# The last 64 rows of the projections' low weights, multiplied for two tiles at once on halves of the array

## The chip, the cores and the metric

The kernel runs on one core of one Trainium2 chip. Its engines work side by side, each through its own queue in order: PE (TensorE, the matrix array, with its weight loads listed apart as PEld), ACT (ScalarE), DVE (VectorE), POOL (GpSimd) and SP (SyncE, which here only issues DMAs). The metric is the device time of one execution in microseconds (us); lower is better. Before the change it is 1898.07 us, the median of three runs (1897.98 to 1898.41).

## The reference

Four blocks over x of 2048 tokens by 448 features, each added to x: attention with 16 heads of 28 features, a gated feed-forward block with 1792 hidden features, and both once more with the same weights.

```python
x = x + attention(layernorm(x), wqkv, wo)
x = x + (sigmoid(g) * u) @ w_down        # g, u = layernorm(x) @ w_gate, w_up
x = x + attention(layernorm(x), wqkv, wo)
x = x + (sigmoid(g) * u) @ w_down
```

The change lies in the first step of attention, `qkv = layernorm(x) @ wqkv`, a product over 448 features that gives 448 columns each for queries, keys and values. It runs twice, once in each layer.

## The kernel before

**Split numbers.** The products run in 16-bit floats, with each operand cut into a high and a low part: hi(w)·hi(x) + hi(w)·lo(x) + lo(w)·hi(x). The 448 features are three blocks of 128 rows and a tail of 64. For the tail one operand holds two things: `tail` has hi(x) in rows 0 to 63 and lo(x) in rows 64 to 127, and the tail's weights stand twice, in rows 0 to 63 and again in rows 64 to 127. One matmul with the high weights gives hi·hi + hi·lo, a second one with the low weights gives lo·hi (and lo·lo). So an output tile takes 3 × 3 + 2 = 11 matmuls.

**Blocks and tiles.** The tokens are cut into four blocks (b = 0 to 3) of 512. For each block `qk(b, ...)` makes seven output tiles of 128 features by 512 tokens: queries and keys, 896 rows in all. Tile i goes into a PSUM bank, one of four in turn. What follows a tile is written out in this order: ACT copies it as 16-bit `hl` (L756), DVE computes the rest (L757), ACT squares it (L759), DVE takes the larger of the two halves' squares (L761), SP stores `hl` to DRAM (L764), and then the tile's entry of the list `fill` is called. That entry is work for later blocks: statistics (`norm`), scaling and transposing (`squares`), storing and reading back (`store`, `gather`), cutting into high and low (`ready`, which is `part` for two row blocks each: L218 and L223 on ACT, L219 and L224 on DVE). Layer 0 has `add` there too, sums of squares of other weights (L957). All of it goes into the same in-order queues of ACT, DVE, POOL and SP.

**The norm products.** Each tile's squares go through a small matmul into a bank of query norms (L735) or key norms (L738). They wait in the queue `late`: from tile 3 on one is taken per tile, and `finish()` (called `fin`) takes those left, three of them, and has DVE reduce the two banks to `peaks` (L774). PE meets `fin` at a place fixed in its program: for layer 0 after the third tile of values of block 1, after the second tile of queries and keys of block 3 (for block 2, through `before`), and after the first tile of values of block 2 (for block 3); for layer 1 after the second tile of values of block 0, and then as in layer 0 (block 1 after its second tile of values).

**Values.** `vals(b, ...)` makes four tiles of 128 tokens by 448 features for a block, 11 matmuls each (L586 to L591), which ACT copies (L792). Block 0's and block 1's come right after their queries and keys; blocks 2 and 3 have theirs after block 3's queries and keys. The third tile of block 3 goes to bank 0 in layer 0 and bank 7 in layer 1, and DVE copies it (L794). Behind it start the scores of attention (L1202), which write groups of three banks each, in a fresh set of banks laid over the same memory.

In layer 0 block 0 is special: its matmuls are interleaved with the making of the weights (`along`), and blocks 0 and 1 are turned on PE (`turned_high`, `turned_low`) instead of through DRAM.

Of the kernel before, what the change touches and what calls it, by code (L numbers as in the profile page):

```python
# [25 lines left out]
NT = S // P  # L26
NB = 4
TB = NT // NB
W = TB * P
# [11 lines left out]
PS = 2.0 ** -13  # L41
# [77 lines left out]
def interleaved_layers(ctx: ExitStack, tc: tile.TileContext, x_in, wqkv, wo, w_gate, w_up,  # L119
                       w_down, out):  # L120
    nc = tc.nc
# [6 lines left out]
    big = Slots(spool, "s", N_SLOTS)  # L128
# [22 lines left out]
    def bank(i, name):  # L151
        return psum(f"bank{i}", name, [P, 512])


    x = cpool.tile([P, NT, D], F32, name="x")
# [62 lines left out]
        nc.scalar.copy(hi, raw)  # L218
        nc.vector.tensor_tensor(lo, raw, hi, op=ALU.subtract)  # L219

    def split_tail(tail, raw):

        nc.scalar.copy(tail[0:64], raw[0:64])  # L223
# [39 lines left out]
    class Block:  # L263
# [97 lines left out]
        def part(self, kt):  # L361

            raw = self.raw[:, kt, :].rearrange("p (i t c) -> p t i c", i=4, t=TB)
            order = "p (t i c) -> p t i c"
            if kt < 3:
                hi = self.hi[:, kt, :].rearrange(order, t=TB, i=4)
                lo = self.lo[:, kt, :].rearrange(order, t=TB, i=4)
                split(hi, lo, raw)
            else:
                split_tail(self.tail.rearrange(order, t=TB, i=4), raw)  # L370
                big.put(self.raw)

        def steps(self):
# [149 lines left out]
        def turned_high(self, kts=range(4), engine=None):  # L523
            for kt in kts:
                if kt not in self.pt:
                    continue
                to, pt = ((self.hi[:, kt, :], self.pt[kt]) if kt < 3 else
                          (self.tail[0:64], self.pt[kt][0:64]))
                if engine is nc.vector:
                    nc.vector.tensor_copy(to, pt)  # L530
                else:
                    nc.scalar.copy(to, pt)

        def turned_low(self, kts=range(4)):
            for kt in kts:
# [13 lines left out]
            else:  # L549
                big.put(self.all)  # L550

    def by_features(pm, blk, wh, wl, first_tile=None):

        order = [(wh, blk.hi), (wh, blk.lo), (wl, blk.hi)]
        terms = [(w(kt), x[:, kt, :]) for kt in range(3) for w, x in order]
        tails = [(w(3), blk.tail) for w in (wh, wl)]
        if first_tile == 0:
            terms = terms[0::3] + terms[1:5:3] + terms[2::3] + terms[7:8] + tails
        elif first_tile == 1:
            terms = terms[0::3] + terms[1::3] + tails[0:1] + terms[2::3] + tails[1:2]  # L560
        else:
            terms += tails
        for i, (w, x) in enumerate(terms):
            nc.tensor.matmul(pm, w, x, start=(i == 0), stop=(i == len(terms) - 1))  # L564

    def of_halves(pm, w, blk, k, first):

# [14 lines left out]
    def by_tokens(pm, hi, lo, tail, w, kts=range(4)):  # L582

        for kt in kts:
            if kt == 3:
                nc.tensor.matmul(pm, tail, w[:, 0, 3, :], start=False, stop=False)  # L586
                nc.tensor.matmul(pm, tail, w[:, 1, 3, :], start=False, stop=True)  # L587
                continue
            nc.tensor.matmul(pm, hi(kt), w[:, 0, kt, :], start=(kt == 0), stop=False)  # L589
            nc.tensor.matmul(pm, hi(kt), w[:, 1, kt, :], start=False, stop=False)  # L590
            nc.tensor.matmul(pm, lo(kt), w[:, 0, kt, :], start=False, stop=False)  # L591
# [120 lines left out]
    def project(layer, wq, begun):  # L712


        values = [big.get("val", [P, TB, H, VC]) for _ in range(NB)]
# [4 lines left out]
                nc.gpsimd.memset(v[:, :, :, DH:DH + 1], 1.0)  # L720

        peaks = cpool.tile([H, 2, NB], F32, name=f"peaks{layer}", tag="peaks", bufs=2)
        evac = [0]

        def qk(b, blk, fill, before):
            pn = [bank(4 + 2 * (b % 2), "qnorm"), bank(5 + 2 * (b % 2), "knorm")]
            late = deque()

            def rows_of_heads(i):

                return ind[:, i:i + P // H, :].rearrange("p a h -> p (a h)")

            def norm_products(i, sq):
                if i <= 3:
                    nc.tensor.matmul(pn[0][:, 0:W // 2], rows_of_heads(i), sq[:, 0:W // 2],  # L735
                                     start=(i == 0), stop=(i == 3))
                if i >= 3:
                    nc.tensor.matmul(pn[1][:, 0:W // 2], rows_of_heads(1 + i), sq[:, 0:W // 2],  # L738
                                     start=(i == 3), stop=(i == 6))
                qrt.put(sq)  # L740

            for i in range(7):
                pm = bank(evac[0] % 4, "qkp")
                evac[0] += 1
                c = slice(i * P, (i + 1) * P)
                by_features(pm, blk, lambda kt: wq.qk[0][:, kt, c],
                            lambda kt: wq.qk[1][:, kt, c], i if layer == 0 and b == 0 else None)
                if layer == 0 and b == 0:
                    along[i]()
                if i == 1 and before:  # L750
                    before()
                if len(late) == 3:
                    late.popleft()()
                hl = qrt.get("qkhl", [P, 2, W], F16)
                sq = qrt.get("sq", [P, W], BF16)
                nc.scalar.activation(hl[:, 0, :], pm, AF.Copy, scale=PS)  # L756
                nc.vector.scalar_tensor_tensor(hl[:, 1, :], pm, PS, hl[:, 0, :], op0=ALU.mult,  # L757
                                               op1=ALU.subtract)
                nc.scalar.activation(sq, hl[:, 0, :], AF.Square)  # L759

                nc.vector.tensor_tensor(sq[:, 0:W // 2], sq[:, 0:W // 2], sq[:, W // 2:W],  # L761
                                        op=ALU.max)
                n = slice(b * W, (b + 1) * W)
                nc.sync.dma_start(qk_scr[c, :, n], hl)  # L764
                qrt.put(hl)
                late.append(lambda i=i, sq=sq: norm_products(i, sq))
                if i < len(fill) and fill[i]:
                    fill[i]()

            def finish():  # L770
                while late:
                    late.popleft()()
                for i in range(2):
                    nc.vector.tensor_reduce(peaks[:, i, b:b + 1], pn[i][0:H, 0:W // 2], axis=AX.X,  # L774
                                            op=ALU.max)
            return finish

        def values_product(pv, blk, j, kts=range(4)):
            t = slice(j * P, (j + 1) * P)
            by_tokens(pv[:, 0:D], lambda kt: blk.hi[:, kt, t], lambda kt: blk.lo[:, kt, t],  # L780
                      blk.tail[:, t], wq.v, kts)

        def vals(b, blk, after, tiles=range(TB), at=None, begun=None):
            for j in tiles:
                pv = begun or bank(evac[0] % 4 if at is None else at, "vp")
                evac[0] += 1
                values_product(pv, blk, j, range(2, 4) if begun else range(4))
                if j in after:
                    after[j]()
                v, pv = values[b][:, j, :, 0:DH], pv[:, 0:D].rearrange("p (h d) -> p h d", d=DH)  # L790
                if at is None:
                    nc.scalar.activation(v, pv, AF.Copy, scale=PS)  # L792
                else:
                    nc.vector.tensor_scalar(v, pv, PS, None, op0=ALU.mult)  # L794
            if tiles[-1] == TB - 1:
                blk.drop()

        def tile0():
            wq.low_cols(0, P, D)
            wq.measure(1)  # L800
            ones_of_values()
# [10 lines left out]
        def nothing():  # L812
# [989 lines left out]
    wq = WeightsQKV()  # L1802
    wq.tiles()
    first = Block(0)
    begun = [first]
# [41 lines left out]
    for layer in range(LAYERS):  # L1847
        values, heads, last_values = project(layer, wq, begun)
        gate = WeightsGated()
        outs = attend(layer, values, heads, last_values, gate, wq.keep)  # L1850
        mlp_first = out_project(outs, gate)
        wq = WeightsQKV()
# [5 lines left out]
        begun = gated(layer, mlp_first, gate, before_next)  # L1858
# [28 lines left out]
```

## Time and profile before

| | us |
|---|---|
| median of three runs | 1898.07 |
| the profiled execution | 1896.41 |
| its span, first to last instruction | 1894.6 |
| PE busy | 1888.2 (100%) |
| DVE busy | 1431.0 (76%) |
| ACT busy | 1383.4 (73%) |
| POOL busy | 231.5 (12%) |
| layer 0, first query/key matmul to first score | 12.43 to 118.35 |
| layer 1, the same | 954.15 to 1056.30 |

A row of the timeline gives the start, the time taken, the engine and source line, the output and input, and how many instructions are merged in the row; square brackets hold the idle time just before and what ended it. Matmuls overlap, so the pitch from one start to the next is what a matmul costs PE, not the time taken that its row shows. A row of the stretches gives, for a piece of the span, its length and each engine's busy time and number of instructions, then the granted PE clock and the load of the DMA engines.

### The profile page before, as it was taken

What the parts mean: (1) busy time and instruction counts of PE and PEld (TensorE: products, weight loads), DVE (VectorE), ACT (ScalarE), POOL (GpSimd) and SP (SyncE); (2) the same over time, 40 slices, a digit from 0 to 9 for tenths busy, and PEclk for the clock granted to TensorE, in tenths of its full rate; (3) what the DMA queues carried; (4) which work ended last, traced back from release to release, by engine and by line L of the source; (5) the groups of instructions that cost most, each with busy time, mean ns of one, the idle gap of its engine ahead of it and who ended that gap; (6) DMA issues with size and microseconds to landing.
All of it is one profiled execution on the core that took longest, in us unless ns stands there. A gap on an engine that the chain in (4) does not pass through costs nothing. (4 is left out here: it accounts for less than half of the span.)

```text
span 1894.6 us, 56258 instructions
## 1 busy us (share of the span) xinstructions
PE 1888.2 (100%) x24254; PEld 1334.2 (70%) x24254; DVE 1431.0 (76%) x2835; ACT 1383.4 (73%) x1772; POOL 231.5 (12%) x453
## 2 busy tenths in 40 slices
PE   9999999999999999999999999999999999999999
PEld 4455555556566799999954566766556677999998
DVE  7758989898976688787563487787778676887664
ACT  5569999999993566555345799999999745665541
POOL 3023112222101111111100000000000020121110
PEclk9999999999999999999999999999999999999999
DMA  7676444344323566646734321122121135666553
GB/s 250 194 212 164 130 137 130 108 118 130 102 81 116 191 205 236 230 182 237 251 97 132 90 52 47 32 52 52 30 49 53 61 127 169 218 253 223 209 208 142
DMA packets 109570, 269.81 MB, mean 142 GB/s; under 512 B 12926, under 2 KB 66526, under 8 KB 109184
## 3 DMA queue, kind: packets, MB, share of 16 engines
q0 software_dynamic: 31776, 158.51, 23.5%
q1 hardware_dynamic: 77200, 107.38, 20.2%
q8 instruction: 192, 3.15, 0.7%
q14 instruction: 66, 0.54, 0.1%
q10 hardware_dynamic: 336, 0.23, 0.0%
HBM read 207.88 MB, written 50.85 MB: 137 GB/s over the span
## 5 line engine op out<-in xcount | busy, mean ns | idle before, releaser
L1217 ACT ACTIVATE prob_s<-sc 128x1536 f32<-128x1536 f32 (+1 forms) x657 | 887.8, 1483 | 6.7 <-PE sc L1202 5.9
L1253 PE MATMUL acc<-prob_s,val_s 128*32 128x256 f32 (+3 forms) x7700 | 571.7, 383 | 0.0
L1202 PE MATMUL sc<-qp_s 114*32 114x512 f16 x7868 | 554.9, 379 | 0.0
L579 PEld LDWEIGHTS <-gu_s 128*128 128x128 f16 x4368 | 426.8, 98 | 46.9
L1202 PEld LDWEIGHTS <-qp_s 114*32 114x32 f16 x8192 | 277.3, 95 | 199.0 <-issue 82.7
L1253 PEld LDWEIGHTS acc<-prob_s,val_s 128*32 128x32 f32 x7700 | 276.7, 110 | 139.2 <-issue 12.4
L579 PE MATMUL chain<-xwide_s,gu_s 128*128 128x256 f16 x2016 | 247.5, 273 | 0.0
L1533 PE MATMUL dnp<-dn_s,hparts_s 128*128 128x224 f16 x2016 | 225.2, 259 | 0.0
L1533 PEld LDWEIGHTS <-hparts_s 128*128 128x128 f16 x2016 | 194.0, 98 | 4.4
L1233 DVE SCALAR_TENSOR_TENSOR power_q<-power_q,expo_q 128x512 f32<-128x512 f32 x243 | 168.2, 692 | 8.3
L1606 ACT COPY one_q<-chain 128x256 f32<-128x256 f32 x224 | 82.4, 371 | 121.1 <-PE chain L579 120.4
L1622 DVE TENSOR_TENSOR one_q<-side,one_q 128x512 f32<-128x512 f32 x112 | 72.2, 687 | 103.3 <-PE side L579 100.7
L579 PE MATMUL side<-xshort_s,gu_s 128*128 128x256 f16 x1120 | 140.6, 273 | 0.0
L564 PE MATMUL qkp<-xhl_s,wqk_s 128*128 128x512 f16 x616 | 137.9, 379 | 0.7 <-ACT wqk_s L231 0.2
L564 PEld LDWEIGHTS <-wqk_s 128*128 128x128 f16 x616 | 60.1, 98 | 70.4 <-ACT wqk_s L231 1.1
L1418 POOL DMA_DIRECT2D gu_s<-gu_parts x104 | 56.0, 538 | 431.9 <-PE side L579 418.1
L1282 DVE STREAM_TRANSPOSE oturned_q<-acc 128x512 f32<-128x512 f32 x32 | 22.9, 716 | 97.0 <-PE acc L1253 96.9
L1253 PE MATMUL acc<-power_q,val_s 128*32 128x256 f32 (+3 forms) x300 | 94.2, 396 | 0.0
L579 PE MATMUL side<-xwide_s,gu_s 128*128 128x256 f16 x672 | 91.7, 273 | 0.0
L1486 ACT CAST hparts_s<-hsums_q 128x256 f16<-128x256 f32 (+1 forms) x136 | 65.0, 494 | 30.1 <-DVE hsums_q L1498 20.4
L756 ACT ACTIVATE qkhl_q<-qkp 128x512 f16<-128x512 f32 x56 | 33.2, 593 | 73.2 <-PE qkp L564 69.6
L1633 ACT ACTIVATE one_q<-one_q 128x512 f32<-128x512 f32 x56 | 35.2, 629 | 63.9 <-DVE one_q L1622 63.9
(218 smaller groups left out, 2333.2 us busy)
## 6 DMA issues: line engine op xcount, KB each, us to landing
gu_s<-gu_parts POOLq DMA_DIRECT2D x104, 800.0 KB, 6.0
dn_s<-dn_parts POOLq DMA_DIRECT2D x42, 784.0 KB, 7.6
qp_s<-qk_scr SPq DMA_DIRECT2D x96, 224.0 KB
qk_scr<-qkhl_q SPq DMA_DIRECT2D x56, 256.0 KB
gu_parts<-pack_s POOLq DMA_DIRECT2D x14, 800.0 KB, 3.8
xt_scr<-xs_s SPq DMA_DIRECT2D x48, 224.0 KB
xraw_s<-xt_scr SPq DMA_DIRECT2D x12, 768.0 KB
qp_s<-qk_scr SPq DMA_DIRECT2D x64, 112.0 KB
```

The lines of the kernel that those rows point to most:

```text
L564: nc.tensor.matmul(pm, w, x, start=(i == 0), stop=(i == len(terms) - 1))
L579: nc.tensor.matmul(pm, a, x, start=(first and i == 0), stop=(i == len(terms) - 1), skip_group_check=True)
L1202: nc.tensor.matmul(ps[32 * j:32 * j + 32, :], hd.k[:, keys], hd.q[:, qb * W:(qb + 1) * W], start=True, stop=True, tile_position=(0, 32 * j))
L1217: nc.scalar.activation(prob[:, 0:n, :], ps[:, 0:n, :], AF.Exp, scale=exp_scale)
L1233: nc.vector.scalar_tensor_tensor(p, p, c[k], y, op0=ALU.add, op1=ALU.mult)
L1253: nc.tensor.matmul(acc[qb * VC:(qb + 1) * VC, s], v[:, kc % TB, h, :], probs[c * NB + qb][:, s], start=(kc == 0 and a == 0), stop=(kc == N ...
L1418: queue.dma_start(self.gu[-1][m], gu_parts[p, m])
L1486: nc.scalar.copy(to[:, :, 0], a)
L1533: nc.tensor.matmul(pm, a[:, x, t], w[:, p, y], start=(begin and n == 0 and (j == 0 or alone)), stop=(n == 2), skip_group_check=True)
L1606: nc.scalar.copy(to, pm)
L1622: nc.vector.tensor_tensor(one[m], side[m], one[m], op=ALU.add)
L1633: nc.scalar.activation(out, v, AF.Sigmoid, scale=gate_scale)
```

## The change

The second tail matmul, with the low weights, needs only hi(x), that is 64 rows. It is now made with 64 rows: for even tiles with rows 0 to 63 (`tail`), for odd tiles with rows 64 to 127, for which a copy of the tail's hi(x) is put into rows 64 to 127 of a new operand `upper`. `on_halves` issues these matmuls for a group of four tiles, even and odd in turn. For that, the first four tiles of queries and keys of a block first get 10 matmuls each, one tile after the other; then come the four half matmuls; then the four tiles' copies with what belongs to them, and only then tiles 4 to 6, with 11 matmuls as before. The same holds for the four tiles of values of a block. Left as they were: queries, keys and values of block 0 in layer 0, and values of block 3.

Four tiles are now open at once, so six banks go round (0 to 3, 6, 7; block 0 of layer 0 keeps four), and both norms of a block share one bank (4 or 5). `late` gives one norm product per tile from tile 4 on, so that four are left for `fin`. The third values tile of block 3 goes to bank 0 in both layers.

```diff
-    def split_tail(tail, raw):
+    def split_tail(tail, upper, raw):
         nc.scalar.copy(tail[0:64], raw[0:64])
+        nc.scalar.copy(upper[64:128], raw[0:64])
         nc.vector.tensor_tensor(tail[64:128], raw[0:64], tail[0:64], op=ALU.subtract)
...
-            self.all = big.get("xhl", [P, 7, W], F16)
+            self.all = big.get("xhl", [P, 8, W], F16)
+            self.upper = self.all[:, 7, :]
...
+                if kt == 3 and self.b > 0:
+                    nc.scalar.copy(self.upper[64:128], pt[0:64])
...
+    def on_halves(outs, high, low):
+        for i, pm in enumerate(outs):
+            r = slice(64 * (i % 2), 64 * (i % 2) + 64)
+            nc.tensor.matmul(pm, *(v[r] for v in (high(i), low(i))), start=False, stop=True)
...
-            terms += tails
+            terms += tails if ends else tails[:1]
...
-        evac = [0]
+        order = deque([0, 1, 2, 3] if layer == 0 else [0, 1, 2, 3, 6, 7])
+        def next_bank(name):
+            order.rotate(-1)
+            return bank(order[-1], name)
+        def alone(b):
+            return layer == 0 and b == 0
...
-            pn = [bank(4 + 2 * (b % 2), "qnorm"), bank(5 + 2 * (b % 2), "knorm")]
+            if layer == 0 and b == 1:
+                order.extend([6, 7])
+            both = bank(4 + b % 2, "norms")
+            pn = [both[:, 0:W // 2], both[:, W // 2:W]]
...
+            def copies(i, pm):
...
                 if i < len(fill) and fill[i]:
                     fill[i]()
+            group = []
+            for i in range(7):
+                pm = next_bank("qkp")
+                c = columns(i)
+                single = alone(b) or i > 3
+                by_features(pm, blk, lambda kt: wq.qk[0][:, kt, c],
+                            lambda kt: wq.qk[1][:, kt, c], i if alone(b) else None, single)
+                if alone(b):
+                    along[i]()
+                if i == 1 and before:
+                    before()
+                if len(late) >= 3:
+                    late.popleft()()
+                if single:
+                    copies(i, pm)
+                    continue
+                group.append(pm)
+                if i == 3:
+                    on_halves(group, lambda i: wq.qk[1][:, 3, columns(i)],
+                              lambda i: blk.upper if i % 2 else blk.tail)
+                    for j, pm in enumerate(group):
+                        copies(j, pm)
...
+            grouped = not alone(b) and b < NB - 1
             for j in tiles:
+                pvs[j] = begun or (next_bank("vp") if at is None else bank(at, "vp"))
+                values_product(pvs[j], blk, j, range(2, 4) if begun else range(4), not grouped)
                 if j in after:
                     after[j]()
+                if not grouped:
+                    copy_values(b, j, pvs[j], at)
+            if grouped:
+                on_halves([pvs[j][:, 0:D] for j in tiles],
+                          lambda j: (blk.upper if j % 2 else blk.tail)[:, j * P:(j + 1) * P],
+                          lambda j: wq.v[:, 1, 3, :])
+                for j in tiles:
+                    copy_values(b, j, pvs[j], at)
...
-        vals(3, blks[3], {}, [2], 0 if layer == 0 else 7)
+        vals(3, blks[3], {}, [2], 0)
```

The inner part of `copies` is the code of L754 to L768, unmoved, the call of `fill[i]` at its end included.

More of the change, by code (lines that the diff above doesn't have):

```diff
@@ L369, in part @@
             else:
-                split_tail(self.tail.rearrange(order, t=TB, i=4), raw)
+                split_tail(self.tail.rearrange(order, t=TB, i=4),
+                           self.upper.rearrange(order, t=TB, i=4), raw)
                 big.put(self.raw)
@@ L561, in by_features @@
         else:
[L562 removed]
+            terms += tails if ends else tails[:1]
         for i, (w, x) in enumerate(terms):
[L564 removed]
+            nc.tensor.matmul(pm, w, x, start=(i == 0), stop=(ends and i == len(terms) - 1))
     def of_halves(pm, w, blk, k, first):
@@ L580, in of_halves, with by_tokens @@
                              stop=(i == len(terms) - 1), skip_group_check=True)
-    def by_tokens(pm, hi, lo, tail, w, kts=range(4)):
+    def by_tokens(pm, hi, lo, tail, w, kts=range(4), ends=True):
         for kt in kts:
@@ L734, in norm_products, with columns @@
                 if i <= 3:
-                    nc.tensor.matmul(pn[0][:, 0:W // 2], rows_of_heads(i), sq[:, 0:W // 2],
-                                     start=(i == 0), stop=(i == 3))
+                    nc.tensor.matmul(pn[0], rows_of_heads(i), sq[:, 0:W // 2],
+                                     start=(i == 0), stop=(i == 3), skip_group_check=True)
                 if i >= 3:
-                    nc.tensor.matmul(pn[1][:, 0:W // 2], rows_of_heads(1 + i), sq[:, 0:W // 2],
-                                     start=(i == 3), stop=(i == 6))
+                    nc.tensor.matmul(pn[1], rows_of_heads(1 + i), sq[:, 0:W // 2],
+                                     start=False, stop=(i == 6), skip_group_check=True)
                 qrt.put(sq)
[L742 to L753, printed above, removed]
+            def columns(i):
+                return slice(i * P, (i + 1) * P)
+            def copies(i, pm):
+                c = columns(i)
                 hl = qrt.get("qkhl", [P, 2, W], F16)
```

26 lines of the change are left out of this document (14 added, 12 removed).

## Prediction

> **What bounds the kernel.** The page comes first: whose time is the span?
>
> ```profile
> PE 1888.2 (100%) x24254; PEld 1334.2 (70%) x24254; DVE 1431.0 (76%) x2835; ACT 1383.4 (73%) x1772; POOL 231.5 (12%) x453
> ```
>
> PE is never free, so a matmul less is time less, and a wait on PE is time more. But 76% for DVE is a mean over the span, so I read next the stretches that the change touches: here the queries and keys of layer 0's block 3, and the whole of layer 1's block 0.
>
> ```profile
> 84.85:105.21 20.36, 20.07 (x102) 9.70 (x100) 19.16 (x41) 11.05 (x20) 0.00 (x0) 1.00 0.37 124
> 954.15:980.29 26.14, 25.97 (x131) 12.63 (x129) 19.64 (x45) 12.28 (x21) 2.43 (x4) 1.00 0.30 89
> ```
>
> The numbers behind the length are PE, PEld, DVE, ACT, POOL. DVE is busy for 19.16 of 20.36 us in the one and 19.64 of 26.14 in the other: in places DVE is a second bound. Third, the timeline of PE at the places where `fin` stands:
>
> ```profile
> 90.27 0.27 PE L738 MATMUL knorm<-sq_q,ind 128*128 128x256 bf16 x1 [0.29 <-DVE sq_q L761]
> ...
> 104.88 0.49 PE L738 MATMUL knorm<-sq_q,ind 128*128 128x256 bf16 x3
> ...
> 975.47 0.38 PE L738 MATMUL knorm<-sq_q,ind 128*128 128x256 bf16 x2
> 976.03 0.27 PE L738 MATMUL knorm<-sq_q,ind 128*128 128x256 bf16 x1 [0.17 <-DVE sq_q L761]
> ```
>
> In two of them PE waits already, 0.29 and 0.17 us, for the last square's maximum on DVE. DVE is just in time there, and the change starts DVE's chain later.
>
> **What it saves on PE.** Pitches first.
>
> ```profile
> 954.15 9.66 PE L564 MATMUL qkp<-xhl_s,wqk_s 128*128 128x512 f16 x44
> ```
> ```profile
> 1058.47 0.35 PE L590 MATMUL vp<-wv_s,xhl_s 128*128 128x448 f16 x1
> 1058.66 0.35 PE L591 MATMUL vp<-wv_s,xhl_s 128*128 128x448 f16 x1
> 1058.95 0.83 PE L1202 MATMUL sc<-qp_s 114*32 114x512 f16 x12
> 1059.71 0.36 PE L589 MATMUL vp<-wv_s,xhl_s 128*128 128x448 f16 x1
> ```
>
> 44 matmuls in 9.66 us, of which the last one's tail is about 0.16, are 0.216 each; a values matmul is 0.19 (1058.66 less 1058.47). The last three rows also show the array changing shape: scores use it in strips of 32 columns. Going in, the first score starts at 1058.95, 0.10 later than the pitch from 1058.66 would have it; coming back, three rounds at 0.216 after 1058.95 end at 1059.60, and the next full matmul starts at 1059.71: 0.11. The twelve scores go in rounds of four side by side.
>
> No row shows halves of rows. A pair of half matmuls costs between one matmul (0.216: side by side) and two (0.432: one after the other). I take the lower end, since four column strips, the nearest row, run side by side. By the Trainium skill ("TensorE: Matmul & The Clock Gate", Part 3, Packing small matmuls) tiles on different rows overlap with about 4 ns between starts; the pair would be 0.22, and the sum as it stands. Changing the shape costs between 0 and the 0.21 above; I take 0.21 per group, since it is a change of shape as those are.
>
> A group of queries and keys turns four matmuls into two pairs: 2 × 0.216 less 0.21 is 0.22 us; there are seven groups (three in layer 0, four in layer 1): 1.6. A group of values: 2 × 0.19 less 0.21 is 0.17; five groups (blocks 1, 2 and then 0, 1, 2): 0.85. Together 2.4 us, 0.13%: that is the whole gain. With free changes of shape it would be 4.9.
>
> **What it moves.** Tile 0 to 3's copies, and the four `fill` entries between them, now wait for the group's end instead of their own tile's. ACT's and DVE's queues are in order, so everything behind moves too. ACT's pitches:
>
> ```profile
> 956.72 0.60 ACT L756 ACTIVATE qkhl_q<-qkp 128x512 f16<-128x512 f32 x1 [28.84 <-PE qkp L564]
> ...
> 988.24 1.14 ACT L218 CAST xhl_s<-xraw_s 128x512 f16<-128x512 f32 x2 [1.74 <-DMA xraw_s<-xt_scr]
> 989.28 0.59 ACT L756 ACTIVATE qkhl_q<-qkp 128x512 f16<-128x512 f32 x1
> 989.90 0.63 ACT L759 ACTIVATE sq_q<-qkhl_q 128x512 bf16<-128x512 f16 x1
> 990.44 0.60 ACT L218 CAST xhl_s<-xraw_s 128x512 f16<-128x512 f32 x1
> 990.95 0.61 ACT L223 CAST xhl_s<-xraw_s 64x512 f16<-64x512 f32 x1
> 991.47 0.58 ACT L756 ACTIVATE qkhl_q<-qkp 128x512 f16<-128x512 f32 x1
> ```
>
> A tile's copy and square are 1.15; two L218 1.04; an L218 and the tail's L223 1.03, to which `upper` adds a copy like L223, 0.51, seven in all, on an ACT that is busy for half of these stretches. A tile's copy begins 0.41 after its last matmul starts (956.72 less 954.15 less ten pitches).
>
> **Layer 1, block 0: the largest term.**
>
> ```profile
> 964.71 0.69 DVE L757 SCALAR_TENSOR_TENSOR qkhl_q<-qkp,qkhl_q 128x512 f16<-128x512 f32 x1
> ...
> 975.13 0.65 DVE L757 SCALAR_TENSOR_TENSOR qkhl_q<-qkp,qkhl_q 128x512 f16<-128x512 f32 x1
> 975.70 0.27 DVE L761 TENSOR_TENSOR sq_q<-sq_q 128x256 bf16<-128x256 bf16 x1
> ```
>
> DVE's work on tile 3 starts at 964.71; behind it stand `b2.norm`, tile 4, two `squares`, tile 5, two `squares`, tile 6, and the last maximum ends at 975.97: 11.3 us with hardly a gap, and after the change the same instructions in the same order. Now when does it start? The group's 40 matmuls end at 954.15 + 8.64; with the change of shape the first half matmul starts at 962.89, tile 0's copy at 963.30. ACT then does tiles 0 and 1 (2.30), two L218 (1.04), tile 2 (1.15), L218, L223 and `upper` (1.54), tile 3's copy (0.60): DVE can start tile 3 at 969.95, 5.2 us later than before. Its chain ends at 981.2. PE asks for it after 962.89 + 0.43 + 0.11, tiles 4 to 6 with a norm product each (3 × 2.48) and two values tiles of ten matmuls (3.8): at 974.7. PE waits 6.5 us, in two gaps (tile 5's norm product comes between). Against the old time the norm product is 5.2 us late; behind it two values tiles took 4.2 us and now take 4.4 (20 matmuls, two pairs, two changes of shape). **Block 0 ends 5.4 us later.**
>
> **The rest of layer 1.** Blocks 1 to 3 have no DVE work between tiles 3 and 6, so ACT sets the pace: tile 6's maximum comes about 0.3 us before PE asks in blocks 1 and 3, and 2 us before in block 2. No wait: −0.4, −0.2, −0.4. Block 2's rows come back from DRAM 5.2 us later, as all before them; the row of 988.24 becomes 993.5, and ACT needs them at 997.1 (two tiles after the group). Then the bank of the third values tile:
>
> ```profile
> 1056.30 0.40 PE L1202 MATMUL sc<-qp_s 114*32 114x512 f16 x4
> ```
> ```profile
> 1056.40 0.62 DVE L794 TENSOR_SCALAR val_s<-vp 128x448 f32<-128x448 f32 x1 [6.18 <-PE vp L587]
> ```
>
> With bank 7 the first score starts while DVE still copies. If the scores' first group lies over bank 0, as its place as the first allocated says, it starts after 1057.02: +0.75 (bounds: 0 and 0.75). Layer 1: 5.4 − 1.0 + 0.75 = **+5.15**.
>
> **Layer 0.** The same with DVE's rows here:
>
> ```profile
> 50.02 0.68 DVE L757 SCALAR_TENSOR_TENSOR qkhl_q<-qkp,qkhl_q 128x512 f16<-128x512 f32 x1
> ...
> 62.63 1.29 DVE L219 TENSOR_TENSOR xhl_s<-xraw_s,xhl_s 128x512 f16<-128x512 f32 x2 [0.57 <-ACT xhl_s L218]
> 63.84 0.69 DVE L757 SCALAR_TENSOR_TENSOR qkhl_q<-qkp,qkhl_q 128x512 f16<-128x512 f32 x1
> ...
> 84.13 2.08 DVE L957 CUSTOM_DVE_ANT_0 junk_s<-raw_s,sums 128x1792 bf16<-128x1792 f32 x1
> ...
> 89.33 0.69 DVE L757 SCALAR_TENSOR_TENSOR qkhl_q<-qkp,qkhl_q 128x512 f16<-128x512 f32 x1
> ...
> 96.79 1.13 DVE L957 CUSTOM_DVE_ANT_0 junk_s<-raw_s,sums 128x896 bf16<-128x896 f32 x1
> ```
> ```profile
> 65.27 0.49 PE L738 MATMUL knorm<-sq_q,ind 128*128 128x256 bf16 x3
> ```
>
> Block 1 (from 41.86): tile 1's DVE work moves from 50.02 to 52.8 (group end 50.6, copy 51.0, one tile 1.15, copy 0.6); of these 2.75 us the 0.57 of waiting before 62.63 and a little more are taken up, tile 6's goes from 63.84 to 65.94, its norm product to 66.9, where PE stood at 65.27 before. With the fourth values tile and its pairs (2.5) the block ends at 69.5 instead of 67.7: **+1.8**.
>
> Block 2: its group ends at 78.2. ACT's row (tiles 0, 1, two L218, tile 2, L218, L223, `upper`, tiles 3, 4) brings tile 4's DVE work to 86.4 and the first `add` from 84.13 to 87.2, 3.07 later. From there it is DVE's old row (two `add` and a tile, 5.2 us, to 89.33), so the last norm product goes from 90.27 to 93.3. PE asks at 90.7, so it waits 2.6. Cumulative **+3.07**.
>
> Block 3: PE leaves `fin` at 93.45; two tiles (4.3) and a change of shape later the group's pairs start at 97.9, tile 0's DVE work at 98.9. Behind it in DVE's queue: tiles 0 to 6 at 0.8 (5.20 less two `add` of 2.2), and three `add` of 2.2, 1.3 and (128 columns more) 1.4: the last maximum at 109.4. PE asks at 107.6, waits 1.8, leaves at 109.55; before, the three products of 104.88 ended their pitches at 105.2. Cumulative **+4.35**; the rest (three values tiles, the start of attention) is as long as before, 6.3 us.
>
> **Free things.** The shared norm bank: PE writes both norms before DVE reads either. Banks: in each place the bank that PE takes next was read by DVE over 1 us before. SP's stores of `hl` come in bunches; the gathers behind them are covered as above, in layer 0's block 2 with 0.7 us to spare.
>
> **Sum.** 4.35 + 5.15 = +9.5 us. The profiled execution had 1896.41 (span 1894.6 and 1.8 around it), 1.66 below the median; added to the median: **1907.6**. What a measurement of this kernel tells from no change is about 0.2%, 3.8 us.
>
> **Rivals.**
> *Not slower (0.07).* DVE has over 6 us to spare in layer 1's block 0 (19.64 of 26.14); if its queue were not held up, PE would ask and find. Then only the 2.4 us gain and the bank's 0.75 stay: 1896.4. It decides at the last maximum of that block: it must end by 974.7, not 981.2. Against it: the spare time lies ahead of the group's end, where DVE has nothing to do.
> *The pairs run one after the other (0.12).* Then 0.43 more in seven groups and 0.38 in five, 4.9: 1912.5. The strips of the scores speak against it.
> *The clock falls in the waits (0.12).*
>
> ```profile
> 1.25 4.88 PE L261 MATMUL still<-still_q 128*128 128x512 f16 x11 [1.25 <-DVE warm L179]
> ```
>
> The first eleven matmuls of the kernel took 4.88 us, where eleven take 2.54 at the pitch above: a PE that comes from rest loses 2.3 us. If the gaps of about 3 us in layer 1's block 0 (and one of 2.6 in layer 0) do this, it is 2.3 to 4.6 more: 1910 to 1912. The Trainium skill ("TensorE: Matmul & The Clock Gate", Part 1) has the clock halved after an idle window of about 3.4 us; by it the gaps, each just about that long and cut by norm products, would mostly escape.
> *Some waits are shorter than worked out (0.09)*: half of them leaves +3 to 4, about 1902.
>
> **How the numbers follow.** The forecast has 0.60: 1907.6, its own range 1904.5 to 1910 (0.75 for the bank, 2 for waits worked out to some tenths each). The range goes from 1903.0 to 1912.8, up to the serial pairs. Slower by over 0.2% (above 1901.9): 0.60 + 0.12 + 0.12 + most of 0.09, and some of the first rival's cases, 0.89; same 0.08; faster, which needs free changes of shape and no wait at all (1893.9), 0.03.
>
> **What the changed profile would show.** In the list of waits, PE for DVE's squares (L761) with 12 to 14 us in all instead of 0.5, the longest gaps of about 3 us in layer 1's block 0. DVE's busy time as before, idle for some 9 us in each block's group. Half matmuls in pairs within 0.22 us, 0.1 us free on either side. The first score of layer 0 some 4.4 us later, that of layer 1 9.5. Wrong would be: norm products without waits, or waits on a DMA or a bank that I called free.

## The result and the profile after

The changed kernel takes 1910.57 us, the median of 6 executions (1908.95 to 1914.19); the kernel before took 1897.82 beside it (1897.32 to 1898.41, 6 executions). The ratio is 1.0068, with a 95% interval of 1.0057 to 1.0078: 12.75 us slower. The forecast was 1907.6, with a range of 1903.0 to 1912.8. The profiled execution has 1911.11 us and a span of 1909.3, 14.7 more than the one of before.

The engines' line of the page, after:

```profile
PE 1889.6 (99%) x24254; PEld 1326.4 (69%) x24254; DVE 1432.0 (75%) x2835; ACT 1382.5 (72%) x1779; POOL 231.4 (12%) x453
```

The work is as before, within 1.5 us on every engine (PE's weight loads, listed apart, take 7.8 us less), and the instructions are as many, but for the seven copies to `upper` on ACT. So nearly all of the 14.7 us is time in which PE stands still; what it does more slowly hides in its busy time, which should have fallen. In the list of PE's waits after, two entries stand out (in all, times, longest):

```profile
PE norms L763 <- DVE sq_q L779: 11.7, 7, 3.4
PE sc L1254 <- DMA qp_s<-qk_scr: 1.3, 1, 1.3
```

The first was 0.5 us before the change, the second was not there. A third entry, PE's wait for the turning of the first tokens (`turn`) at the kernel's start, has 1.0 us instead of 0.2; it lies between 0.2 and 2.0 us in the twelve traces and is 1.6 us in experiment 7, which is the kernel before with `fin` moved, so it is no part of the change. Where do the seven waits of the first entry stand? The timeline of PE, the norm products that waited and the rows behind two of them:

```profile
65.33 0.27 PE L763 MATMUL norms<-sq_q,ind 128*128 128x256 bf16 x1 [0.20 <-DVE sq_q L779]
67.33 0.27 PE L763 MATMUL norms<-sq_q,ind 128*128 128x256 bf16 x1 [1.74 <-DVE sq_q L779]
67.44 0.35 PE L603 MATMUL vp<-wv_s,xhl_s 128*128 128x448 f16 x1
67.63 0.54 PE L604 MATMUL vp<-wv_s,xhl_s 128*128 128x448 f16 x1
...
71.08 0.55 PE L562 MATMUL vp<-wv_s,xhl_s 64*128 64x448 f16 x4
...
95.78 0.27 PE L763 MATMUL norms<-sq_q,ind 128*128 128x256 bf16 x1 [2.56 <-DVE sq_q L779]
...
111.21 0.27 PE L763 MATMUL norms<-sq_q,ind 128*128 128x256 bf16 x1 [0.53 <-DVE sq_q L779]
112.01 0.27 PE L763 MATMUL norms<-sq_q,ind 128*128 128x256 bf16 x1 [0.53 <-DVE sq_q L779]
...
984.75 0.27 PE L763 MATMUL norms<-sq_q,ind 128*128 128x256 bf16 x1 [3.44 <-DVE sq_q L779]
987.70 0.37 PE L763 MATMUL norms<-sq_q,ind 128*128 128x256 bf16 x1 [2.68 <-DVE sq_q L779]
987.87 0.58 PE L603 MATMUL vp<-wv_s,xhl_s 128*128 128x448 f16 x1
988.24 0.58 PE L604 MATMUL vp<-wv_s,xhl_s 128*128 128x448 f16 x1
...
992.70 0.35 PE L603 MATMUL vp<-wv_s,xhl_s 128*128 128x448 f16 x1
992.89 0.35 PE L604 MATMUL vp<-wv_s,xhl_s 128*128 128x448 f16 x1
```

They are the `fin` of blocks 1, 2 and 3 of layer 0 and of block 0 of layer 1, the places that the prediction named. But read on behind the waits: from 987.87 the values matmuls follow each other at 0.373 us instead of 0.19, for thirteen of them, until 992.70. The same from 67.63 to 71.08. In the stretches (length, then PE, PEld, DVE, ACT, POOL, then the granted clock, the third number from the end):

```profile
66.00:72.00 6.00, 4.67 (x17) 1.67 (x17) 3.31 (x7) 1.14 (x3) 0.00 (x0) 0.72 0.77 196
88.30:112.12 23.82, 20.20 (x102) 9.39 (x100) 20.60 (x44) 12.26 (x22) 0.00 (x0) 1.00 0.30 100
960.27:994.61 34.34, 28.22 (x132) 12.54 (x130) 22.18 (x50) 10.80 (x20) 2.43 (x4) 0.90 0.29 81
```

The clock fell to half for some microseconds behind the waits of layer 0's block 1 and layer 1's block 0 (0.72 and 0.90 as means over the stretch), and not behind the 2.56 us of block 2 (1.00). The last two rows answer to the two stretches of before: 23.82 us against 20.36 for layer 0's block 3, 34.34 against 26.14 for layer 1's block 0.

The half matmuls, in layer 0's block 1:

```profile
49.14 1.89 PE L576 MATMUL qkp<-xhl_s,wqk_s 128*128 128x512 f16 x8
50.96 0.60 PE L562 MATMUL qkp<-xhl_s,wqk_s 64*128 64x512 f16 x4
51.50 0.82 PE L576 MATMUL qkp<-xhl_s,wqk_s 128*128 128x512 f16 x3
```

In shorter stretches of the timeline the four stand in two rows, one for each pair:

```profile
50.96 0.39 PE L562 MATMUL qkp<-xhl_s,wqk_s 64*128 64x512 f16 x2
```
```profile
51.19 0.38 PE L562 MATMUL qkp<-xhl_s,wqk_s 64*128 64x512 f16 x2
```

Two matmuls that start at 50.96 and take 0.39 us together, no longer than one, run side by side; the second pair starts 0.23 us later. The eight end their pitches at 49.14 + 8 × 0.216 = 50.87, and the next full matmul starts at 51.50: the four halves with both changes of shape take 0.63 us, where four full matmuls take 0.86. That is a saving of 0.23, where 0.22 was forecast.

### The profile page after: what moved, and what is told of

Same layout as the page of the kernel before. It is cut to its first block, busy times and chain, and to the rows that moved or that the text cites. A ratio compares the mean times of both kernels' runs of the same rounds, so it can differ in the third digit from the quotient of the medians.

```text
span 1909.3 us, 56265 instructions
## 1 busy us (share of the span) xinstructions
PE 1889.6 (99%) x24254; PEld 1326.4 (69%) x24254; DVE 1432.0 (75%) x2835; ACT 1382.5 (72%) x1779; POOL 231.4 (12%) x453
## 5 line engine op out<-in xcount | busy, mean ns | idle before, releaser
L576 PE MATMUL qkp<-xhl_s,wqk_s 128*128 128x512 f16 x588 | 132.2, 380 | 0.7 <-ACT wqk_s L232 0.2
L775 DVE SCALAR_TENSOR_TENSOR qkhl_q<-qkp,qkhl_q 128x512 f16<-128x512 f32 x56 | 38.3, 685 | 57.6 <-ACT qkhl_q L774 57.6
```

The lines of the kernel that those rows point to most:

```text
L576: nc.tensor.matmul(pm, w, x, start=(i == 0), stop=(ends and i == len(terms) - 1))
```

## The experiments

**1. Four tiles at once, but whole rows.** Is it the grouping that costs, or the half matmuls?

```diff
-            r = slice(64 * (i % 2), 64 * (i % 2) + 64)
-            nc.tensor.matmul(pm, *(v[r] for v in (high(i), low(i))), start=False, stop=True)
+            nc.tensor.matmul(pm, high(i), low(i), start=False, stop=True)
...
-                              lambda i: blk.upper if i % 2 else blk.tail)
+                              lambda i: blk.tail)
```

(The values' operand is changed alike.)

> The groups of four stay, but the matmuls with the tail's low weights use all 128 rows again, as before the change, so the array never changes its shape. Theory A (the time goes into PE's waits for DVE's maxima, because the copies and the fill entries moved behind the group): nothing of that is undone, the groups end about 0.2 us later, so about 2 us more than the changed kernel, 1911 to 1914, with the same waits of PE for the squares, 10 to 14 us in all. Rival B (half matmuls and changes of shape are what costs): the loss goes, 1897 to 1900, and the waits for the squares with it.

Measured: 1912.02 us (1910.59 to 1912.80), ratio 1.0078 [1.0061, 1.0094]. PE's waits in its profile:

```profile
PE norms L762 <- DVE sq_q L778: 10.6, 6, 3.2
```

Without a single half matmul the loss is all there, with waits at the same places: the loss is the grouping's. The half matmuls are no part of it.

**2. `fin` later.** The norm products that PE waits for are asked for behind the next block's first four tiles, 4 us (block 2) to 13 us later in the block's time; the reductions to `peaks`, which are part of `fin`, move along, and nothing else does.

```diff
-                if i == 1 and before:
+                if i == 3 and before:
...
-            along_values = {0: b3.norm, 1: lambda: (fin(), sq(3, 0, 1)()), 2: b2.gather,
+            along_values = {0: b3.norm, 1: sq(3, 0, 1), 2: b2.gather,
...
-        fin = qk(1, b1, fill, None)
-        vals(1, b1, {0: b3.gather, 2 if layer == 0 else 1: fin})
+        fin = qk(1, b1, fill, fin if layer > 0 else None)
+        vals(1, b1, {0: b3.gather})
...
-                         add], None)
+                         add], fin)
```

> Only the place moves where PE asks for the last four norm products: those of layer 0's block 1 and layer 1's blocks 0 and 1 go from the block's own values into the next block's queries and keys, after its fourth tile, and those of block 2 from the second to the fourth tile of block 3. Half matmuls, groups, copies and DVE's order stay. Theory A: the waits for the squares fall from 11.7 us to about 2 (only layer 0's block 3 keeps its wait), the half-speed stretches behind two of them (about 4 us) go too: 1896 to 1899. Rival B: the time stays above 1908. Rival C (DVE's and the gathers' lateness is felt wherever it is asked for): the waits come back at other places, on a bank, the next block's rows or the norm products, and the time stays above 1904.

Measured: 1897.05 us (1896.19 to 1898.74), ratio 0.9999 [0.9989, 1.0008]. What is left of the two waits:

```profile
PE sc L1254 <- DMA qp_s<-qk_scr: 1.3, 1, 1.3
PE norms L763 <- DVE sq_q L779: 1.1, 2, 0.5
```

DVE does the same work, and but for the reductions to `peaks` in the same order; PE asks later. 13.5 us of the changed kernel's time go, more than the 10.6 us of waits that went; the rest fits the half clock, which is gone with them (the granted clock is 1.00 throughout). The 2.4 us that remain in the two rows above are as much as the halves were to save, and the kernel is as long as before the change. The loss stood at the places of `fin`.

**3. The gaps filled.** Useless matmuls, 14 and 11 in the two gaps of layer 1's block 0 and 7 in that of layer 0's block 1, with PE still waiting for the same squares.

```diff
+            def warm_up(n):
+                pm = bank(5 - b % 2, "still")
+                for _ in range(n):
+                    nc.tensor.matmul(pm, wq.qk[0][:, 0, 0:P], blk.hi[:, 0, :], start=True, stop=True)
+
             def finish():
+                spare = {(0, 1): (0, 0, 0, 7), (1, 0): (0, 0, 14, 11)}.get((layer, b), (0,) * 4)
+                for n in spare[-len(late):] if late else ():
+                    if n:
+                        warm_up(n)
+                    late.popleft()()
```

> Added work: matmuls into a bank that nobody reads, put into three of the gaps in which PE waits for DVE: 14 and 11 of 512 columns (3.0 and 2.4 us) in layer 1's block 0 and 7 (1.5 us) in layer 0's block 1. All else is the changed kernel. If PE's clock falls because PE stands still, the half-speed stretches after these gaps go (1.7 and 2.4 us): 1906 to 1908 in spite of 32 matmuls more. If the slow matmuls have another cause, the time stays at 1910.6 or rises.

Measured: 1908.55 us (1906.72 to 1910.48), ratio 1.0057 [1.0040, 1.0074]. The stretch around the gaps of layer 1's block 0 in after, and then both stretches in this kernel (after's first is shown above, with 0.72):

```profile
984.00:995.00 11.00, 7.57 (x28) 3.02 (x28) 9.91 (x24) 0.48 (x2) 1.20 (x2) 0.69 0.55 132
```
```profile
66.00:72.00 6.00, 5.78 (x31) 2.46 (x29) 3.32 (x7) 2.98 (x6) 0.00 (x0) 1.00 0.78 194
984.00:995.00 11.00, 10.26 (x52) 4.58 (x51) 9.94 (x24) 1.85 (x4) 1.20 (x2) 1.00 0.54 133
```

With PE busy in the gaps the clock stays at 1.00 behind them, and the kernel with 32 matmuls more is 2 us shorter. That the fall goes is shown by the stretches; the medians' 2 us are less firm, as the executions of the two kernels overlap, and the median lies half a microsecond above the forecast 1906 to 1908. The same trace has the counterpart: the gap of layer 0's block 2 (2.58 us here) was left empty, and behind it the clock did fall, which it had not done in the changed kernel's trace (the rows stand in the last section).

**4. Another bank for the third values tile.** In layer 1 it goes to bank 5, which the scores' first group does not take.

```diff
-        vals(3, blks[3], {}, [2], 0)
+        vals(3, blks[3], {}, [2], 0 if layer == 0 else 5)
```

> The third values tile of layer 1's block 3 goes to bank 5 instead of bank 0. If the first score of layer 1 waits because its banks lie over bank 0, which DVE is still copying, the 1.3 us of waiting before it go, 1909.3 or so, and the first score starts about 0.1 us after the pitch of the last values matmul. If it waits for a transfer of the head's rows, as the profile has it, the 1.3 us stay: 1910.6.

Measured: 1909.33 us (1908.39 to 1912.32), ratio 1.0067 [1.0050, 1.0083]. Timelines of PE and of DVE at the first score of layer 1, after, and then in this kernel:

```profile
1070.88 0.83 PE L1254 MATMUL sc<-qp_s 114*32 114x512 f16 x12 [1.29 <-DMA qp_s<-qk_scr]
```
```profile
1069.63 0.62 DVE L848 TENSOR_SCALAR val_s<-vp 128x448 f32<-128x448 f32 x1 [6.67 <-PE vp L601]
```
```profile
1068.01 0.35 PE L601 MATMUL vp<-wv_s,xhl_s 128*128 128x448 f16 x1
1068.29 1.62 PE L1254 MATMUL sc<-qp_s 114*32 114x512 f16 x24
```
```profile
1068.40 0.62 DVE L848 TENSOR_SCALAR val_s<-vp 128x448 f32<-128x448 f32 x1 [6.66 <-PE vp L601]
```

After, the first score comes 0.63 us after DVE's copy is done; here it starts ahead of the copy, 0.09 us behind the pitch of the last values matmul, which is the price of the change of shape. The edit leaves the loads as they were. So the 1.29 us were the bank, though the profile names a DMA as what ended the wait. The other traces bear it out: the wait stands, with 1.0 to 1.3 us, in all five that have bank 0 there (after, experiments 1, 2, 3 and 8), and in none of the five with bank 5 (4, 5, 6, 9 and 10). What fills the 0.63 us between the end of the copy and the score isn't shown. The 1.2 us between the medians agree, but lie within their spread.

**5. All at once, with the sums out of the way.** Experiments 2 and 4 together, and the three `add` of layer 0's block 3 put behind `worst_of_heads`, where DVE is idle.

```diff
-        fin = qk(3, blks[3], [add, add, add], fin)
+        fin = qk(3, blks[3], [], fin)
...
-        vals(2, blks[2], {0: guard_of_norms, 3: worst_of_heads})
+        def worst_and_sums():
+            worst_of_heads()
+            if layer == 0:
+                for _ in range(3):
+                    tell.add()
+
+        vals(2, blks[2], {0: guard_of_norms, 3: worst_and_sums})
```

> The half matmuls with all three hindrances taken away: PE asks for the norm products in the next block, the third values tile of layer 1 goes to bank 5, and the three sums of squares (add) of layer 0's block 3 come after the worst of the heads, when DVE has nothing else. Nothing is left out of the work. If the account is complete, PE waits nowhere for a square or a bank and the 2.4 us that the half matmuls save are left, with the 0.5 us that PE waited before the change: 2.4 to 2.9 us less than before, 1894.5 to 1895.0. If something else is lost with the groups (ACT's burst, the stores in bunches, more load on the transfers), it stays at 1896 to 1898.

Measured: 1904.60 us (1902.53 to 1906.57), ratio 1.0037 [1.0023, 1.0051]: a miss. In PE's timeline stands one wait, and in DVE's what it was for:

```profile
123.38 0.55 PE L603 MATMUL vp<-wv_s,xhl_s 128*128 128x448 f16 x1 [8.14 <-DVEq L958]
```
```profile
110.71 0.20 DVE L945 TENSOR_SCALAR flag<-worst,back 1x1 int32<-1x1 f32 x1
110.84 2.06 DVE L1015 CUSTOM_DVE_ANT_0 junk_s<-raw_s,sums 128x1792 bf16<-128x1792 f32 x1
...
115.88 0.15 DVE L1019 COPY sums<-part 128x1 f32<-128x1 f32 x1
```

Behind `worst_of_heads` the program branches on `flag` (L958), and each engine has a branch there in its own queue; PE's next matmul waits until DVE is past it. DVE's instructions of that line (the first start of each stands before "to"):

```profile
L958 DVEq COMPARE_BRANCH  x2: 68/70/72, 116.5 to 1057.8; - x2
L958 DVEq EVENT_SEMAPHORE  x2: 21/21/21, 123.3 to 1060.7; - x2
```

With 5.2 us of sums ahead of it in its queue, DVE comes to the branch at 116.5, and PE, which stands ready from 115.24 on, goes on only after DVE's next instruction at 123.3. In experiment 9, which differs in the place of the sums alone, DVE branches at 110.9, its next instruction comes at 114.0, and PE doesn't wait there. So DVE's idle time at this place was no place for the sums. Why DVE takes 6.8 us to get past the branch here and 3.1 us there isn't shown. Behind the wait PE's clock is halved as well (123.38 has a matmul of 0.55 us).

**6. The same with whole rows.** Experiment 5 with both edits of experiment 1:

```diff
+            nc.tensor.matmul(pm, high(i), low(i), start=False, stop=True)
```

> The same kernel, but with the tail's low weights on all 128 rows: it measures the half matmuls by themselves, without any wait around them. By pitches (14 pairs of queries and keys, 10 of values, two changes of shape at 0.1 us for each of 12 groups) it should be 2.4 us slower than the kernel with halves, about 1897.2. If the pairs ran one after the other, both kernels would differ by 2.5 us the other way; if changes of shape were free, by 4.9.

Measured: 1905.04 us (1903.13 to 1906.13), ratio 1.0041 [1.0028, 1.0055]. It waits 6.3 us at the same branch, and experiment 5 waits 8.1, so the difference of 0.4 between the two says nothing about the half matmuls.

**7. The kernel before, with `fin` later.** The edit of experiment 2 in the kernel before: does it bring time by itself?

```diff
-                if i == 1 and before:
+                if i == 3 and before:
```

(With the other lines of experiment 2.)

> The kernel before, with only the places moved where PE asks for the norm products, as in the two above. There are 0.5 us of waiting to win: 1896.9. If it gains 2 us or more, the gain of the kernels above is not that of the half matmuls.

Measured: 1896.28 us (1896.02 to 1899.28, 11 executions) against 1897.35 (1896.76 to 1898.96), ratio 0.9997 [0.9988, 1.0006]. The kernel before had its squares just in time; asking later brings no difference that can be told.

**8. More work for DVE.** Four useless copies (1.64 us together) in DVE's chain of layer 1's block 0, ahead of the last two maxima.

```diff
-                    lambda: b2.squares([0, 1]), sq(2, 2, 3), b2.store]
+                    lambda: (b2.squares([0, 1]), more()), sq(2, 2, 3), b2.store]
...
+            def more():
+                junk = qrt.get("junk", [P, D])
+                for _ in range(4):
+                    nc.vector.tensor_copy(junk, x[:, 0, :])
+                qrt.put(junk)
```

> The changed kernel with four useless copies of 448 columns on DVE (about 2 us) in layer 1's block 0, behind the two squares between tiles 4 and 5. If DVE's queue behind the group is what PE waits for there, the two gaps of 3.4 and 2.7 us grow by the copies' whole time, to about 8 us together, and the norm products' waits in all to about 13.7 us. If PE waits for something else, less.

Measured, one execution: 1911.59 us. The two waits of block 0:

```profile
986.29 0.37 PE L763 MATMUL norms<-sq_q,ind 128*128 128x256 bf16 x1 [5.03 <-DVE sq_q L779]
989.24 0.37 PE L763 MATMUL norms<-sq_q,ind 128*128 128x256 bf16 x1 [2.58 <-DVE sq_q L779]
```

5.03 + 2.58 instead of 3.44 + 2.68: 1.5 us more wait for 1.64 us more work (the copies are shorter than the 2 us counted on, and the waits for squares are 13.2 us in all, with 13.7 forecast). DVE's chain is what sets the end of this block, about one to one.

**9. The sums in a real gap.** Experiments 2 and 4, and three `add` put ahead of block 2's copies, where DVE waits for the group anyway.

```diff
-                         add], fin)
-        fin = qk(3, blks[3], [add, add, add], fin)
+                         add], lambda fin=fin: (add and [add() for _ in range(3)], fin()))
+        fin = qk(3, blks[3], [], fin)
```

> The changed kernel with the three `fin` of the second run moved past the next block's first four tiles, the third values tile of the last block of layer 1 in bank 5, and three of the six `add` of layer 0 (2.3 us of VectorE each) moved from the last block to before block 2's four copies, where VectorE stands idle from 69.1 to 77.0 in the second run's trace. Theory A (VectorE's queue behind a group is what TensorE waits for): the second run had 1897.05; the bank gives 1.3, and the last block's two waits of 0.53 go, so about 1894.7, some 2.7 us and 0.14% below the kernel before. Rival (the sums only move the wait: block 2's own copies come late behind them, or the sums wait for their rows): 1895.8 or more, with a wait of over 1 us for block 2's squares or values.

Measured: 1894.21 us (1893.66 to 1895.02, 11 executions) against 1897.36 (1896.50 to 1899.69, 21 executions), ratio 0.9983 [0.9974, 0.9992]: faster than both kernels, by 0.17% against the one before, and within the forecast of its theory A. PE's list of waits holds no score and, for squares, 0.2 us; DVE's timeline shows the sums in the gap, with 0.95 us to spare:

```profile
PE norms L760 <- DVE sq_q L779: 0.2, 1, 0.2
```
```profile
68.35 2.08 DVE L1009 CUSTOM_DVE_ANT_0 junk_s<-raw_s,sums 128x1792 bf16<-128x1792 f32 x1
...
75.11 0.15 DVE L1013 COPY sums<-part 128x1 f32<-128x1 f32 x1
76.22 0.74 DVE L815 TENSOR_REDUCE peaks<-norms 16x1 f32<-16x256 f32 x2 [0.95 <-PE norms L763]
```

**10. The same with whole rows.** Experiment 9 with both edits of experiment 1:

```diff
+            nc.tensor.matmul(pm, high(i), low(i), start=False, stop=True)
```

> The same as the kernel above, but the last rows' matmuls whole, one tile after the other, as before the change. With no waits left in the projections on either side, this difference is what the half matmuls are worth by themselves: 0.22 in each of 7 groups of queries and keys and 0.17 in each of 5 groups of values, 2.4 us, so about 1897.1, as long as the kernel before. If the halves' gain is eaten by VectorE (each group comes to its copies sooner and finds them no sooner done), the two agree within 1 us.

Measured: 1896.31 us (1895.92 to 1896.69, 11 executions), ratio 0.9993 [0.9984, 1.0002]. No execution of this kernel is as short as the longest of experiment 9. The half matmuls alone are worth 2.10 us, with 2.4 worked out. Against the kernel before, this one shows no difference that can be told: with `fin`, the bank and the sums moved, the grouping neither costs nor brings anything by itself.

## Why the prediction was right, and where it was short

The mechanism was right, and so was the direction; the number owes something to luck. 1910.57 lies outside the likeliest case's own range (1904.5 to 1910) and inside that of a rival with a chance of 0.12, the fall of the clock (1910 to 1912), which came on top of the waits. The stated range reaches that far only because it was drawn out to the serial pairs, which did not come.

**Right: what it saves.** 0.23 us in a group of queries and keys was measured in the trace (0.22 worked out), and the whole gain in experiments 9 and 10: 2.10 of 2.4. The column strips of the scores, four side by side, were the right row to take the pair from, and their changes of shape (0.10 and 0.11) the right price for the new ones. The rival of pairs one after the other, 4.9 us, is false.

**Right: where it is lost, and why.** That the loss stands at `fin`, because four tiles' work reaches ACT and DVE only when the group ends and comes through in order, is shown by experiment 2 (it goes when PE asks later), by 1 (it stays without halves) and by 8 (it grows with DVE's chain). DVE's rows of layer 1's block 0, after:

```profile
970.05 0.69 DVE L775 SCALAR_TENSOR_TENSOR qkhl_q<-qkp,qkhl_q 128x512 f16<-128x512 f32 x1 [9.13 <-ACT qkhl_q L774]
...
976.33 0.69 DVE L775 SCALAR_TENSOR_TENSOR qkhl_q<-qkp,qkhl_q 128x512 f16<-128x512 f32 x1 [0.37 <-ACT qkhl_q L774]
...
987.38 0.27 DVE L779 TENSOR_TENSOR sq_q<-sq_q 128x256 bf16<-128x256 bf16 x1
```

The block starts at 960.27. DVE is idle for 9.13 us while the group runs, comes to tile 3 16.06 us into the block (worked out: 15.80) and ends its last maximum at 27.38 (27.05). PE asks at 21.04 (20.55) and waits 3.44 + 2.68 = 6.1 us (6.5). The rival "not slower", which counted on DVE's spare time, fails for the reason given against it: the spare time lies ahead of the group's end.

**Short: the clock.** The likeliest case held the clock at 1.00 and left its fall to a rival with 0.12, at 2.3 us each time. In the profiled execution it fell twice. Layer 1: 13 matmuls at 0.373 instead of 0.19 are 2.4 us. Layer 0: from 67.44 to 71.08 ten matmuls took 3.64, where they took 1.98 with the clock up in experiment 4's trace: 1.7 us. The size was right, the chance was wrong. It rested on the sentence that the Trainium skill ("TensorE: Matmul & The Clock Gate", Part 1) gives, that the clock is halved after an idle window of about 3.4 us, and on the norm products that cut the gaps. The runs disagree: a gap of 1.74 us was enough in some executions, and single small matmuls between 3.44 and 2.68 us of rest did not keep the clock up. The last section shows what decides it.

**Mis-sized: the rest.** In the profiled pair the span grew by 14.7 where 9.5 was the sum; its terms, worked out, and measured as differences of starts in PE's two timelines:

| term | worked out | measured |
|---|---|---|
| start of layer 0's block 1 | 0 | 0.4 |
| layer 0, block 1, without the clock | 1.8 | 1.85 |
| layer 0, block 2 | 1.27 | 1.6 |
| layer 0, block 3 | 1.28 | 1.4 |
| between `fin` of block 3 and layer 1 | 0 | −0.8 |
| layer 1, block 0, without the clock | 5.4 | 5.8 |
| layer 1, blocks 1 to 3 | −1.0 | −1.0 |
| layer 1, bank 0 | 0.75 | 1.3 |
| clock, twice | 0 | 4.1 |
| sum | 9.5 | 14.65 |

The bank's upper bound counted only until the copy ended; the 0.63 us from there to the first score were missing from it. The −0.8 between `fin` of block 3 and layer 1 hides part of the shortfall: 0.17 of it is the group of block 2's values, and the rest, in attention and the gated block, isn't explained. Between the medians, 12.75 us apart, the sum is short by 3.25. That is less than the profiled pair shows: the profiled execution of before lies 1.4 us below its median, and a fall in layer 0 doesn't come in every execution.

**What was to be seen.** The six banks that go round and the shared norm bank were free, as forecast: no wait on them is in the list. The waits for squares, forecast as 12 to 14 us, are 11.7. The first score comes 6.8 us later in layer 0 (4.4 forecast) and 14.6 later in layer 1 (9.5): the terms of the table up to there.

## What to carry to other kernels

Holding back the copies of several tiles until a group is complete cost PE nothing that can be told by itself (experiment 10). It cost most of the 12.75 us where a later instruction on PE asked for the end of the chain behind the copies; asking later won 13.5 us back. Work out when that chain ends, and let PE ask for it later. Here the 2 us saved in matmuls showed only after that move, a free bank and a better place for the sums. And price a new wait of about 2 us or more on PE with the half clock that can follow it, 1.7 to 2.4 us here.

## What the runs showed of the hardware

**A short rest can halve the clock; where it falls decides.** The wait of 1.74 us in layer 0's block 1 (1.73 in experiment 8) was followed by the half rate in after and in experiment 8 (mean clock 0.72 from 66 to 72 us), and not in experiments 1 and 4 (1.00). The gap in layer 0's block 2 (2.2 to 2.6 us in the five traces) was followed by it in experiment 3 alone. The gaps of layer 1's block 0 were followed by it in after and in experiments 1, 4 and 8 (0.69 from 984 to 995).

The granted clock explains the difference. In each of the twelve traces its changes lie whole multiples of 3.413 us apart; behind the waits it stays at half for one such window (after, from 67.66), two (after, from 985.85) or three (experiment 5, from 117.25). Windows cut on that grid, from after, experiment 1 and experiment 3:

```profile
64.25:67.66 3.41, 1.48 (x10) 0.81 (x9) 3.41 (x9) 2.32 (x5) 0.00 (x0) 1.00 0.46 154
67.66:71.07 3.41, 3.41 (x10) 1.12 (x8) 1.65 (x4) 0.00 (x0) 0.00 (x0) 0.50 0.80 187
```
```profile
65.71:69.12 3.41, 1.71 (x10) 0.96 (x10) 3.35 (x8) 1.16 (x3) 0.00 (x0) 1.00 0.64 213
69.13:72.54 3.41, 3.41 (x18) 1.57 (x17) 0.32 (x1) 1.85 (x4) 0.00 (x0) 1.00 0.98 204
```
```profile
90.36:93.77 3.41, 1.22 (x8) 0.66 (x7) 3.38 (x6) 0.00 (x0) 0.00 (x0) 1.00 0.22 77
93.77:97.18 3.41, 3.02 (x8) 1.13 (x8) 3.14 (x7) 0.00 (x0) 0.00 (x0) 0.50 0.23 79
```

In after, the 1.74 us and the 0.20 us before it fall into one window, PE is idle for 1.94 of 3.41 us, and the next window has half the clock. In experiment 1 only 1.70 us of the same rest fall into one window, in experiment 4 1.63, and the clock stays. The gap of block 2 is cut into 1.75 and 0.81 us in after, where nothing follows; in experiment 3, 2.19 us lie in one window. Over all twelve traces, every window at full clock with 1.94 us of rest or more was followed by half the clock, and none with 1.75 or less; at half the clock, 1.85 us of rest kept it there. The matmuls' own rows agree (0.58 us instead of 0.35). The grid lies elsewhere against the program in each execution, so the same rest halves the clock in some and not in others. The Trainium skill ("TensorE: Matmul & The Clock Gate", Part 1) says that the activity window is free-running. The traces agree.

**A change of the array's shape between full rows and 64 rows** costs about what one between full columns and strips of 32 costs, 0.2 us both ways together: 0.63 us less two pairs of 0.216. The Trainium skill ("TensorEngine Tiling (Array Packing)", Tiling Modes, Key Properties) says that changing the mode drains the array, without a figure; the trace agrees that it isn't free.
